# Dense block of a two-layer transformer kernel: sums of inner values all by VectorE, squares by ScalarE, bias rows added in the second half, row statistics one row ahead

## The chip, the cores and the metric

The kernel runs on one core of one Trainium2 chip. The metric is the time of one execution on the device in microseconds (us); before the change it is 3569.39 us, the median of three runs (3567.62 to 3571.59). The engines are named as in the profile: PE is TensorE (matrix products), PEld its weight loads, DVE is VectorE, ACT is ScalarE, POOL is GpSimd, and SP is the queue that issues nearly all transfers (DMAs) between the chip's memory and on-chip memory. Each engine takes its instructions strictly in the order in which the program put them there.

## The reference

All values are float32. Two layers with the same weights run one after the other on x of 2048 rows by 640:

```python
x = x + attention(layernorm(x), wqkv, wo)          # 32 heads of 20
x = x + dense(layernorm(x), w1, b1, w2, b2)

def dense(x, w1, b1, w2, b2):                      # w1: 640 x 1536, w2: 1536 x 640
    h = x @ w1 + b1
    r = where(h > 0, h, 0)
    return (r * r) @ w2 + b2
```

`layernorm` takes a row's mean and variance off and has no weights of its own. So the inner values of the dense part are the squares of what the rectifier lets through, and the bias b2 is a row that is added to every output row.

## The kernel before, in words

PE's operands here are of the type float32r. The kernel splits every operand into a high part (a copy to that type, made by ACT) and a low part (what the copy left out, a subtraction by DVE), and makes three products of each: high-high, high-low, low-high. `split_to` (L322) issues the two instructions.

A layer has three stages: projections to queries, keys and values (`qkv`), `attention`, and what follows here. `add_heads` multiplies the attention's output with wo for four blocks of 512 rows and adds the rows. Then come eight calls of `mlp`, called **blocks** below: `fh` 0 and 1 are the two halves of the 1536 inner columns (first half, second half), and `qb` 0 to 3 are the blocks of 512 rows. The order is fh 0 with qb 0 to 3, then fh 1 with qb 0 to 3; I number them block 0 to block 7 of their layer.

A block has two parts. In the **up** part PE makes six chains of 15 products (L361), one for each 128 inner columns; after each, ACT adds b1 and rectifies (L1454), and DVE squares in place (L1455). After every second chain a **pair** p (0, 1, 2) is complete: `left_operands` makes the left operands of a fast matrix product with seven products in place of eight: sums of quarters of the two squared tiles (L1434 to L1437, four instructions that depend on one another, two for s1 and two for s2), and the splits into high and low of a quarter (`ha`), of the second tile (`h`) and of the sums (`hs`, twice: s1 and s2). In the **y** part PE runs 126 products (L1481) of these operands with w2. It begins with 36 products that need pairs 0 and 1 alone, then takes pair 2: first six products with `ha`, then with s1, with h, and the rest. DVE adds each result to the rows (L1500), 14 instructions.

Beside its own work a block carries **side** work: `side()` is called before the chains, after each of the six chains, once more, and after each of the 14 additions, and each call pops one list of steps that `plan` filled by number (`put(gen, -1, 0, 2)` runs the next step of a generator at those places; -1 is the place ahead of the chains). Two generators matter. `turn_out` normalises four tiles of 128 rows for a later block: statistics (L312, L313 on DVE, then two tiny instructions on POOL, L315 and L316, the second a power), normalisation on DVE (L320), a transposing step on DVE (L1387), and a store to the transposed buffer `d_t` (four DMAs). `turn_in` loads that buffer as columns and splits it (L1403, L1404). In blocks 0 and 1 of both layers `turn_out` runs for a block two further on, and in blocks 5, 6 and 7 of the first layer for the second layer's projections. In block 7 of the first layer the last four row tiles stay on chip: `rows_3` holds their normalised values, which PE transposes early in the second layer (L476).

The order of each engine's instructions is the order in which this Python code issues them; what is waited for follows from the data and from the buffers: 11 buffers for rows (`xtile`) and 42 for operands (`slot`), each reused once its last reader is done. Bias rows: in the first half the four row tiles of x come from the layer's middle rows, and POOL adds b2 to each (L1466); in the second half they come from `d_half`, what the first half stored.

## Time and profile before

| what | us |
|---|---|
| median of three runs | 3569.39 |
| the profiled execution, whole | 3574.83 |
| its span from first to last instruction | 3573.0 |
| PE busy in the span | 3461.2 |
| DVE, ACT, POOL busy | 2864.7, 2640.3, 975.4 |
| the eight blocks of layer one, from their first product | 1416.9 to 1805.7 |
| the eight blocks of layer two | 3204.2 to 3569.6 |
| a block without a wait on PE (layer two, block 5) | 38.9 |

The profiled execution is one run; it took 5.4 us more than the median, and what is summed below is a difference within it. A row of the view of stretches gives a stretch's borders and length, then for PE, PEld, DVE, ACT and POOL the busy time with the number of instructions, then the clock that PE was granted (1.00 is full), the busy share of the transfer engines and GB/s. A row of the timeline gives start, duration, engine, line, operation and tiles, and in brackets the idle time just before it with what ended it. A row of the view of groups gives the count, the busy time and the mean duration in ns, then the idle time before.

### The profile page before, as it was taken

To read this page: it belongs to the slowest core of one execution; us is meant where nothing else is said; L and a number is where in the kernel's file an instruction comes from. 1 tells how busy PE (TensorE), PEld (TensorE's weight loads), DVE (VectorE), ACT (ScalarE), POOL (GpSimd) and SP (SyncE) were. 2 spreads that over 40 slices of the span, in tenths; PEclk is the share of its full clock that TensorE was granted. 3 is DMA by queue.
4 is the path that set the end of the run, shared out by engine and by line. 5 is a ranking of instruction groups with operands and counts; after the bars stand their busy time and mean duration, and the time that the engine had idled before them with its cause. 6 is when DMAs were issued, how large, how long until landed. Compare 5 with 4: busy or idle time off the path is not lost. (4 is left out here: it accounts for less than half of the span.)

```text
span 3573.0 us, 70330 instructions
## 1 busy us (share of the span) xinstructions
PE 3461.2 (97%) x26202; PEld 2163.7 (61%) x26202; DVE 2864.7 (80%) x5341; ACT 2640.3 (74%) x4266; POOL 975.4 (27%) x1128
## 2 busy tenths in 40 slices
PE   9999999999999999799999999999999999997999
PEld 7896444444444438688879964444444444386888
DVE  8888999999999954565668889999999999545654
ACT  3778999999999990232237799999999999902322
POOL 6531355412221120331244201221122211203321
PEclk9999999999999999899999999999999999998999
DMA  9866555422221148756587652222222111487552
GB/s 307 287 223 176 174 170 165 153 65 79 63 54 31 51 152 272 236 207 226 159 268 274 208 158 79 67 85 65 65 79 63 53 31 51 148 275 226 198 220 107
DMA packets 405512, 533.22 MB, mean 149 GB/s; under 512 B 179764, under 2 KB 227380, under 8 KB 405168
## 3 DMA queue, kind: packets, MB, share of 16 engines
q1 hardware_dynamic: 404352, 526.35, 47.0%
q8 instruction: 206, 3.38, 0.4%
q10 hardware_dynamic: 816, 2.36, 0.2%
q14 instruction: 138, 1.13, 0.1%
HBM read 316.59 MB, written 211.98 MB: 148 GB/s over the span
## 5 line engine op out<-in xcount | busy, mean ns | idle before, releaser
L561 DVE TENSOR_REDUCE mx<-banks 128x1 f32<-128x512 f32 x2096 | 1429.0, 686 | 139.5 <-PE banks L549 39.7
L549 PE MATMUL banks<-k,q 60*128 60x512 f32 (+1 forms) x4488 | 1312.3, 371 | 2.0 <-DVE v L445 1.9
L549 PEld LDWEIGHTS banks<-k,q 60*128 60x128 f32 x4488 | 715.0, 184 | 832.2 <-DVE mx L596 725.3
L684 ACT ACTIVATE e<-banks 128x512 f32<-128x512 f32 x1988 | 1194.2, 601 | 16.7 <-PE banks L676 3.6
L690 PE MATMUL banks<-e,vg 128*32 128x512 f32 x8192 | 1093.5, 606 | 1.5 <-ACT e L1295 1.5
L676 PE MATMUL banks<-q,k 62*128 62x512 f32 x3968 | 1074.4, 421 | 0.6 <-DVE mx L617 0.6
L686 ACT ACTIVATE e<-banks 128x1024 f32<-128x1024 f32 x990 | 1007.1, 1017 | 0.0
L596 DVE TENSOR_REDUCE mx<-banks 128x2 f32<-128x512 f32 x928 | 633.0, 682 | 3.3 <-PE banks L549 3.3
L676 PEld LDWEIGHTS banks<-q,k 62*128 62x128 f32 x3968 | 579.9, 184 | 53.8 <-ACT e L684 52.0
L617 DVE CUSTOM_DVE_ANT_0 rl<-banks,rl 128x512 f32<-128x512 f32 x536 | 349.9, 689 | 78.2 <-PE banks L549 56.9
L399 PE MATMUL banks<-xnT,wqk 64*128 64x512 f32 x2400 | 374.6, 394 | 2.3 <-DVE x L1500 1.3
L609 ACT ACTIVATE rl<-banks 128x512 f32<-128x512 f32 x538 | 295.8, 595 | 101.3 <-PE banks L549 85.5
L361 PE MATMUL banks<-xnT,w 128*128 128x512 f32 x1440 | 335.6, 394 | 8.2 <-DVE xnT L1404 8.2
L690 PEld LDWEIGHTS banks<-e,vg 128*32 128x32 f32 x8192 | 161.2, 108 | 261.8 <-issue 257.7
L399 PEld LDWEIGHTS banks<-xnT,wqk 64*128 64x128 f32 x2400 | 297.5, 186 | 32.0 <-issue 2.2
L361 PEld LDWEIGHTS banks<-xnT,w 128*128 128x128 f32 x1440 | 273.0, 190 | 66.3 <-DVE xnT L1404 10.1
L339 POOL CAST mr<-nt 128x32 fp32r<-128x32 f32 x64 | 13.5, 211 | 1086.9 <-DVE nt L643 1086.9
L1454 ACT ACTIVATE r<-banks,b_t 128x512 f32<-128x512 f32 x96 | 64.0, 686 | 301.7 <-PE banks L361 282.2
L734 POOL TENSOR_TENSOR few<-few,minus_t 128x16 f32<-128x16 f32 x62 | 179.9, 2901 | 200.5 <-DMA few<-d_s 200.3
L399 PE MATMUL banks<-wv,xnT 64*128 64x320 f32 x1920 | 209.9, 307 | 0.7 <-ACT mark_t L401 0.7
L399 PEld LDWEIGHTS banks<-wv,xnT 64*128 64x128 f32 x1920 | 202.2, 186 | 1.8 <-ACT mark_t L401 1.4
L549 PE MATMUL banks<-kd,q 60*128 60x512 f32 x538 | 193.4, 397 | 0.0
(111 smaller groups left out, 2969.9 us busy)
## 6 DMA issues: line engine op xcount, KB each, us to landing
q<-d_qk SPq DMA_DIRECT2D x240, 240.0 KB
d_qk<-ev SPq DMA_DIRECT2D x80, 512.0 KB
k<-d_qk SPq DMA_DIRECT2D x152, 240.0 KB
w<-d_w SPq DMA_DIRECT2D x56, 480.0 KB
x<-d_x SPq DMA_DIRECT2D x84, 320.0 KB
d_qk<-ev SPq DMA_DIRECT2D x80, 256.0 KB
d_xn<-xnT SPq DMA_DIRECT2D x40, 512.0 KB
xnT<-d_xn SPq DMA_DIRECT2D x40, 512.0 KB
```

The lines of the kernel that those rows point to most:

```text
L361: nc.tensor.matmul(dst, a, b, start=(n == 0), stop=(n == last))
L399: m = nc.tensor.matmul(ch["dst"][:, :width], *pair, start=first, stop=last)
L549: return nc.tensor.matmul(dst, q_t[t][b : b + 60, p, sub * P : (sub + 1) * P], k_t[t // NQB, c][b : b + 60, p, keys], start=True, stop=True,)
L561: nc.vector.tensor_reduce(maxima(t)[:, 2 * par + p, sub, c : c + 1], dst, axis=AX.X, op=ALU.max)
L596: r = nc.vector.tensor_reduce(maxima(t)[:, p : p + 3 : 2, sub, c if not half else column(t, p, sub)], bank.rearrange("q (r k) -> q r k", r=2),
L609: nc.scalar.activation(res, dst, AF.Relu)
L617: nc.vector.tensor_tensor_reduce(out=r, in0=dst, in1=r, scale=1.0, scalar=LEAST, op0=ALU.add, op1=ALU.max, accum_out=maxima(t)[:, 2 * par ...
L676: nc.tensor.matmul(dst, k_t[t // NQB, kt // 4][b : b + 62, p, (kt % 4) * P : (kt % 4 + 1) * P], q_t[t][b : b + 62, p, :], start=True, stop ...
L684: nc.scalar.activation(es[h], dst, AF.Exp, scale=SCALE)
L686: nc.scalar.activation(es[pair], banks[:, 1:3, :], AF.Exp, scale=SCALE)
L690: nc.tensor.matmul(acc[32 * h : 32 * h + 32, :], v_t[t // NQB, kt // 8][:, kt % 8, 32 * h : 32 * h + 32], es[h], start=(kt == 0), stop=(kt ...
L734: nc.gpsimd.tensor_tensor(few, few, minus_t, op=ALU.pow)
```

## The change

- **Sums.** The four sums of a pair (L1434 to L1437) are issued on DVE for every pair. Before, only pair 2 had them on DVE, and pairs 0 and 1 had them on POOL.
- **Squares.** The square is an activation on ACT (`Square`, in place, right after the rectifier) in place of DVE's product.
- **The quarter `ha`.** Its split is issued right after the first chain of a pair (`upper`), no longer among the pair's other splits; the three other splits take their buffers one by one.
- **Bias rows.** `tensor_add(x, x, b2_t)` on POOL runs in the second half's blocks, no longer in the first half's.
- **Statistics.** `turn_out` takes the statistics of row tile i+1 before it normalises tile i, and has 7 steps in place of 10; the places in `plan` are new. In blocks 0 and 1 the four tiles are done by side place 4 (before, the fourth's normalisation stood at place 13) and stored by place 5; the first two rows of the following `turn_out` are loaded at place 17 in place of 18. In blocks 5 to 7 of layer one the last store stands at place 7.
- **`rows_3`.** In the first layer's block 7 the statistics of tiles 0 and 1 stay at their place; all normalisations, and the statistics of tiles 2 and 3, stand behind the last addition.

```diff
+        mvs = [stats(xs[0])]
+        yield
         for i in range(4):
             if y is not None:
                 store(i - 1)
-            mv = stats(xs[i])
-            yield
-            normalise(nc.vector, xs[i], mv)
+            if i < 3:
+                mvs.append(stats(xs[i + 1]))
+            normalise(nc.vector, xs[i], mvs[i])
             y = xtile("y")
             nc.vector.transpose(y, xs[i])
...
-        def left_operands(p, r, h):
-
-            eng = nc.vector if p == 2 else nc.gpsimd
+        def upper(p, r):
+
             if p % 2 == 0:
                 ops["a", p // 2] = slot([P, 2, QB], F32R, "ha")
             a = ops["a", p // 2][:, :, p % 2 * w : p % 2 * w + w]
-            ops["s1", p] = slot([P, 2, QB], F32R, "hs")
-            ops["s2", p] = slot([P, 2, QB], F32R, "hs")
-            ops["h", p] = slot([P, 2, QB], F32R, "h")
+            split_to(a[:, 0, :], a[:, 1, :], r[:, :w])
+
+        def left_operands(p, r, h):
+
             s = slot([P, 2, 2, w], F32, "s")
             a11, a21, a12, a22 = r[:, :w], r[:, w:], h[:, :w], h[:, w:]
-            eng.tensor_add(s[:, 0, 0, :], a21, a22)
-            eng.tensor_sub(s[:, 0, 1, :], s[:, 0, 0, :], a11)
-            eng.tensor_sub(s[:, 1, 0, :], a12, s[:, 0, 1, :])
-            eng.tensor_sub(s[:, 1, 1, :], a11, a21)
-            split_to(a[:, 0, :], a[:, 1, :], a11)
-            for x, y in (("h", h), ("s1", s[:, 0]), ("s2", s[:, 1])):
-                x = ops[x, p]
+            nc.vector.tensor_add(s[:, 0, 0, :], a21, a22)
+            nc.vector.tensor_sub(s[:, 0, 1, :], s[:, 0, 0, :], a11)
+            nc.vector.tensor_sub(s[:, 1, 0, :], a12, s[:, 0, 1, :])
+            nc.vector.tensor_sub(s[:, 1, 1, :], a11, a21)
+            for key, y in (("h", h), ("s1", s[:, 0]), ("s2", s[:, 1])):
+                x = ops[key, p] = slot([P, 2, QB], F32R, "hs")
                 y = y if y is h else y.rearrange("p a t -> p (a t)")
                 split_to(x[:, 0, :], x[:, 1, :], y)
...
             nc.scalar.activation(r, dst, AF.Relu, bias=b1_t[:, f : f + 1])
-            nc.vector.tensor_mul(r, r, r)
+            nc.scalar.activation(r, r, AF.Square)
             if low:
                 left_operands(p, top, r)
                 top = None
             else:
                 top = r
+                upper(p, r)
...
                 x = row_tile(d_half if fh else x_mid, qb * 4 + n - 1)
-                if not fh:
+                if fh:
                     nc.gpsimd.tensor_add(x, x, b2_t)
...
                     if final and not last:
-                        rows_3.append((x, stats(x)))
-                        if i:
-                            rows_3[i - 1] = to_normal(*rows_3[i - 1])
+                        rows_3.append((x, stats(x) if j == 4 else None))
...
+        for i, (x, mv) in enumerate(rows_3[:]):
+            if i == 3:
+                rows_3[i] = x, stats(x)
+            else:
+                rows_3[i] = to_normal(x, mv or stats(x))
+        x = None
...
-                    (out_0, range(10)), (out_1, range(9, 19)), (in_0, (12, 16, 17, 18, 19, 20))
+                    (out_0, range(7)), (out_1, (9, 10, 11, 13, 15, 17, 18)), (in_0, (8, 12, 14, 16, 18, 19))
...
-                put(outs.pop(0), -1, -1, 0, 0, 2, 2, 4, 13, 14)
+                put(outs.pop(0), -1, -1, 0, 2, 4, 5)
...
-                put(outs[0], 18)
+                put(outs[0], 17)
...
-                at = (6, 8, 9) if qb + 1 == NQB else (13, 15, 16)
-                put(turn_out(d_t[1 + qb], rows_of(x_e, qb - 1)), -1, 0, 0, 2, 2, 4, 4, *at)
+                put(turn_out(d_t[1 + qb], rows_of(x_e, qb - 1)), -1, 0, 0, 2, 4, 6, 7)
```

How this moves instructions is best seen in the built programs. In the lists `r` is a squared tile, `s` the sums, `ha`, `h` and `hs` the split operands, `x` a row tile, `bst` and `mv` its statistics, `y` its transposed or normalised form; the numbers tell tiles apart. New line numbers are two higher than old ones from L1385 on.

**DVE, layer one, block 5, the last pair of the up part.** Before:

```order
L1455 TENSOR_TENSOR r_18262<-r_18262 128x512
L312 BN_STATS bst_18271<-x_18136 128x6 x2
L313 BN_AGGR mv_18272<-bst_18271 128x2
L320 TENSOR_SCALAR x_18136<-x_18136,mv_18272 128x640
L1387 STREAM_TRANSPOSE y_18279<-x_18136 128x640
L1455 TENSOR_TENSOR r_18296<-r_18296 128x512
L1434 TENSOR_TENSOR s_18303<-r_18262,r_18296 128x256
L1435 TENSOR_TENSOR s_18303<-s_18303,r_18262 128x256
L1436 TENSOR_TENSOR s_18303<-r_18296,s_18303 128x256
L1437 TENSOR_TENSOR s_18303<-r_18262 128x256
L325 TENSOR_TENSOR ha_18299<-r_18262,ha_18299 128x256
L325 TENSOR_TENSOR h_18302<-r_18296,h_18302 128x512
```

With the change:

```order
L325 TENSOR_TENSOR ha_18263<-r_18260,ha_18263 128x256
L312 BN_STATS bst_18273<-x_18208 128x6 x2
L313 BN_AGGR mv_18274<-bst_18273 128x2
L320 TENSOR_SCALAR x_18134<-x_18134,mv_18199 128x640
L1389 STREAM_TRANSPOSE y_18281<-x_18134 128x640
L1436 TENSOR_TENSOR s_18301<-r_18260,r_18298 128x256
L1437 TENSOR_TENSOR s_18301<-s_18301,r_18260 128x256
L1438 TENSOR_TENSOR s_18301<-r_18298,s_18301 128x256
L1439 TENSOR_TENSOR s_18301<-r_18260 128x256
L325 TENSOR_TENSOR hs_18306<-r_18298,hs_18306 128x512
L325 TENSOR_TENSOR hs_18309<-s_18301,hs_18309 128x512
L325 TENSOR_TENSOR hs_18312<-s_18301,hs_18312 128x512
```

The two squares are gone from DVE, `ha` stands ahead of the row work, and the normalisation (L320) uses an `mv` of an earlier step, no longer the one just above it.

**DVE, layer two, the beginning of block 1.** Before:

```order
L312 BN_STATS bst_35143<-x_35112 128x6 x2
L313 BN_AGGR mv_35144<-bst_35143 128x2
L320 TENSOR_SCALAR x_35112<-x_35112,mv_35144 128x640
L1387 STREAM_TRANSPOSE y_35151<-x_35112 128x640
L1455 TENSOR_TENSOR r_35170<-r_35170 128x512
L312 BN_STATS bst_35177<-x_35114 128x6 x2
L313 BN_AGGR mv_35178<-bst_35177 128x2
L320 TENSOR_SCALAR x_35114<-x_35114,mv_35178 128x640
L1387 STREAM_TRANSPOSE y_35185<-x_35114 128x640
L1455 TENSOR_TENSOR r_35204<-r_35204 128x512
L325 TENSOR_TENSOR ha_35207<-r_35170,ha_35207 128x256
L325 TENSOR_TENSOR h_35210<-r_35204,h_35210 128x512
```

With the change:

```order
L312 BN_STATS bst_35139<-x_35098 128x6 x2
L313 BN_AGGR mv_35140<-bst_35139 128x2
L312 BN_STATS bst_35146<-x_35100 128x6 x2
L313 BN_AGGR mv_35147<-bst_35146 128x2
L320 TENSOR_SCALAR x_35098<-x_35098,mv_35140 128x640
L1389 STREAM_TRANSPOSE y_35154<-x_35098 128x640
L325 TENSOR_TENSOR ha_35176<-r_35173,ha_35176 128x256
L312 BN_STATS bst_35183<-x_35156 128x6 x2
L313 BN_AGGR mv_35184<-bst_35183 128x2
L320 TENSOR_SCALAR x_35100<-x_35100,mv_35147 128x640
L1389 STREAM_TRANSPOSE y_35191<-x_35100 128x640
L1436 TENSOR_TENSOR s_35213<-r_35173,r_35210 128x256
```

The statistics of the third row tile (`x_35156`) now stand ahead of the first pair's sums; before, they stood behind that pair's splits.

**DVE, layer one, the end of block 7** (`xnT_19392` is the next stage's first split). Before:

```order
L1414 TENSOR_SCALAR y_19270<-x_18961,mv_19232 128x640
L1404 TENSOR_TENSOR xnT_19119<-xnT_19119 128x512
L1500 TENSOR_TENSOR x_19033<-banks,x_19033 128x320
L1500 TENSOR_TENSOR x_19053<-banks,x_19053 128x320
L1500 TENSOR_TENSOR x_19033<-banks,x_19033 128x320
L312 BN_STATS bst_19313<-x_19033 128x6 x2
L313 BN_AGGR mv_19314<-bst_19313 128x2
L1414 TENSOR_SCALAR y_19320<-x_18981,mv_19264 128x640
L1500 TENSOR_TENSOR x_19053<-banks,x_19053 128x320
L312 BN_STATS bst_19335<-x_19053 128x6 x2
L313 BN_AGGR mv_19336<-bst_19335 128x2
L1414 TENSOR_SCALAR y_19342<-x_19033,mv_19314 128x640
```

With the change:

```order
L1502 TENSOR_TENSOR x_19038<-banks,x_19038 128x320
L1502 TENSOR_TENSOR x_19062<-banks,x_19062 128x320
L1416 TENSOR_SCALAR y_19330<-x_18964,mv_19232 128x640
L1416 TENSOR_SCALAR y_19332<-x_18987,mv_19264 128x640
L312 BN_STATS bst_19334<-x_19038 128x6 x2
L313 BN_AGGR mv_19335<-bst_19334 128x2
L1416 TENSOR_SCALAR y_19341<-x_19038,mv_19335 128x640
L312 BN_STATS bst_19343<-x_19062 128x6 x2
L313 BN_AGGR mv_19344<-bst_19343 128x2
L1416 TENSOR_SCALAR y_19358<-x_19062,mv_19344 128x640
L325 TENSOR_TENSOR xnT_19392<-banks,xnT_19392 128x512
```

The additions (L1500, now L1502) no longer have statistics and normalisations between them, and each normalisation of tiles 2 and 3 stands right behind the statistics that it uses.

## The prediction

> **What bounds the kernel now.** The change moves instructions in the dense blocks and in the rows around them alone, so I read the view of stretches first, one stretch for each block with a loss, and one without.
>
> ```profile
> 1416.90:1491.60 74.70, 48.85 (x219) 41.55 (x218) 41.06 (x77) 13.71 (x24) 18.49 (x22) 0.77 0.77 230
> 1491.60:1539.60 48.00, 42.29 (x218) 37.46 (x218) 33.37 (x61) 12.99 (x23) 17.64 (x20) 0.93 0.62 184
> 1539.60:1580.90 41.30, 39.58 (x218) 35.36 (x217) 26.04 (x41) 13.12 (x23) 14.59 (x12) 1.00 0.43 160
> 1580.90:1624.50 43.60, 41.24 (x219) 36.93 (x218) 24.15 (x36) 10.52 (x18) 14.89 (x12) 0.96 0.98 372
> 1663.40:1710.00 46.60, 41.51 (x218) 37.57 (x217) 28.50 (x56) 10.40 (x18) 10.55 (x16) 0.93 0.60 170
> 1710.00:1757.20 47.20, 42.12 (x219) 38.25 (x218) 30.80 (x60) 13.48 (x23) 10.54 (x16) 0.93 0.68 195
> 1757.20:1807.00 49.80, 41.17 (x217) 36.78 (x216) 35.96 (x74) 16.59 (x28) 14.87 (x23) 0.97 0.64 178
> 3204.20:3280.10 75.90, 48.17 (x219) 41.23 (x218) 41.14 (x77) 13.71 (x24) 18.49 (x22) 0.78 0.75 225
> 3280.10:3328.90 48.80, 41.62 (x218) 36.77 (x217) 33.34 (x61) 12.99 (x23) 17.57 (x20) 0.97 0.62 181
> 3328.90:3371.80 42.90, 41.18 (x219) 36.97 (x218) 26.14 (x41) 13.12 (x23) 14.59 (x12) 0.96 0.43 154
> 3371.80:3413.80 42.00, 39.64 (x218) 35.32 (x217) 24.00 (x36) 10.51 (x18) 15.08 (x12) 1.00 1.01 388
> 3452.80:3491.70 38.90, 38.90 (x218) 35.37 (x217) 19.38 (x36) 10.63 (x18) 7.58 (x8) 1.00 0.39 136
> ```
>
> The last row is a block in which PE never waits: 38.9 us. Every other block pays its length less 38.9. Layer one: 35.8, 9.1, 2.4, 4.7 (blocks 0 to 3), 7.7, 8.3, 10.9 (5 to 7; the last up to the next stage's first product). Layer two: 37.0, 9.9, 4.0, 3.1. Together 132.9 us, all that the change can win. Part is idle PE, part a clock below 1.00 after it: with 46.6 us and 41.51 busy, block 5 loses 5.1 by waiting and 2.6 by slow products.
>
> Next the timeline of block 5, PE first, then DVE.
>
> ```profile
> 1663.39 20.59 PE L361 MATMUL banks<-xnT,w 128*128 128x512 f32 x90
> ...
> 1689.14 0.56 PE L1481 MATMUL banks<-w,ha 128*128 128x320 f32 x2
> 1694.79 1.43 PE L1481 MATMUL banks<-w,ha 128*128 128x320 f32 x4 [5.09 <-DVE ha L325]
> ```
>
> ```profile
> 1687.97 0.68 DVE L1455 TENSOR_TENSOR r<-r 128x512 f32<-128x512 f32 x1
> 1688.57 0.88 DVE L312 BATCH_NORM_STATS2 bst<-x 128x6 f32<-128x320 f32 x2
> 1689.48 0.21 DVE L313 BATCH_NORM_AGGREGATE mv<-bst 128x2 f32<-128x12 f32 x1
> 1690.62 0.61 DVE L320 TENSOR_SCALAR x<-x,mv 128x640 f32<-128x640 f32 x1 [0.93 <-POOL mv L316]
> 1691.27 0.84 DVE L1387 STREAM_TRANSPOSE y<-x 128x640 f32<-128x640 f32 x1
> 1692.04 0.65 DVE L1455 TENSOR_TENSOR r<-r 128x512 f32<-128x512 f32 x1
> ...
> 1694.32 0.42 DVE L325 TENSOR_TENSOR ha<-r,ha 128x256 fp32r<-128x256 f32 x1
> ```
>
> PE begins pair 2 at 25.75 us of the block (1689.14 less 1663.39) and stands until `ha` of pair 2 is there. The bound is DVE's order: between the two squares stand a row's statistics, a 0.93 us round trip to POOL, the normalisation and the transposing step. Everything of pair 2, on ACT too, waits for them.
>
> **The change, part by part.** Prices come from the undisturbed block (3452.8 to 3491.7), the view of groups:
>
> ```profile
> L1454 ACT ACTIVATE r<-banks,b_t 128x512 f32<-128x512 f32 x6 | 4.1, 688 | 21.0 <-PE banks L361 20.9
> L324 ACT CAST hs<-s 128x512 fp32r<-128x512 f32 x6 | 3.7, 621 | 6.1 <-POOL s L1435 2.9 <-POOL s L1437 2.7 <-DVE s L1435 0.3
> L1455 DVE TENSOR_TENSOR r<-r 128x512 f32<-128x512 f32 x6 | 4.1, 690 | 6.5 <-ACT r L1454 6.4
> L325 DVE TENSOR_TENSOR hs<-s,hs 128x512 fp32r<-128x512 f32 x6 | 4.1, 689 | 5.1 <-ACT hs L324 5.1
> L1435 DVE TENSOR_TENSOR s<-s,r 128x256 f32<-128x256 f32 x1 | 0.4, 424 | 0.0
> L1435 POOL TENSOR_TENSOR s<-s,r 128x256 f32<-128x256 f32 x2 | 2.1, 1068 | 0.2
> ```
>
> *Squares.* DVE loses six instructions of 0.69 us a block (4.1 us). ACT gains six. No row shows a square on ACT; the nearest are the copy (0.62) and the rectifier with its bias (0.69), and I take 0.65, as it has no tile of biases. ACT then works 10.6 + 3.9 = 14.5 of 38.9 us. This hides beside PE except behind the last chain, where it takes the place of DVE's square. The Trainium skill ("ScalarE: Activation LUTs", the rules for kernel authors) speaks against this part: an element-wise product belongs on VectorE. It gives an ACTIVATE with immediate operands 186 ns + 0.833 ns an element, an estimate of 613 ns for 512. The rows show no dearer engine here (0.62 to 0.69 against 0.69), so the sum is the same by either, and DVE, not ACT, is late.
>
> *Sums.* DVE gains eight instructions a block at 0.42 (3.4 us), about what it lost. The four of a pair take 1.6 us (from 1692.04 + 0.65 to 1694.32, with their waits) where one alone takes POOL 1.07. Before, ACT's `hs` copies waited for POOL; now they wait for DVE. Behind them on ACT stands the next rectifier, and behind that PE's banks, of which eight cover several chains.
>
> *Row statistics ahead.* Nothing is added; the wait for POOL's power (0.93) falls under the next statistics (1.09).
>
> *A block with row work in the second half (5, 6, 7).* Chains end every 3.43 us (20.59/6). The fifth ends at 17.2, `ha` is done near 19.7 (rectify, square, copy, subtract), the row work of side 4 takes 0.88 + 0.21 + 0.61 + 0.84 = 2.5, until 22.2. The last chain's square is there at 20.6 + 0.7 + 0.65 = 22.0. Sums until 23.8, `h` low 24.5, s1 low 25.2. PE wants s1 at 25.75 + 6 products of 0.147 ((38.9 - 20.4)/126) = 26.6. Slack 1.4: no wait. I leave 0.5 us for a collision with POOL. Gains: 7.2 and 7.8.
>
> *Blocks 2 and 3*, no row work: s1 low near 25.0; all of 2.4 + 4.7 + 4.0 + 3.1 = 14.2 goes.
>
> *Blocks 1.* Here the moved statistics meet a transfer. SP (layer two) and what it brings:
>
> ```profile
> 3285.82 1.20 SPq L76 DMA_DIRECT2D x<-d_x  x1
> ...
> 3290.94 1.46 SPq L76 DMA_DIRECT2D x<-d_x  x3
> ```
>
> ```profile
> 3296.76 3.08 POOL L1466 TENSOR_TENSOR x<-x,b_t 128x640 f32<-128x640 f32 x2 [3.25 <-DMA x<-d_x]
> ```
>
> The third tile's load is issued 5.7 us into the block, and the flight of such a load is 5.3 to 5.8 (3290.94 to 3296.76, a bias row of the three), so it lands near 11.0. DVE's statistics of it now stand ahead of pair 0's sums and wait from about 5.8; behind them on DVE queue all the pairs, and PE waits for those. From 11.0 DVE has three row steps (1.1 + 1.45, 1.1 + 1.45, 1.45), three sets of sums (4.8), two sets of three splits (4.0), `ha` twice with ACT's copy (1.9), and the last `h` and s1 (1.3): 18.55, until 29.6. PE wants it at 26.6, so 3 us are lost, and 9.1 + 9.9 - 6 = 13.0 is won. A flight of 3.7 wins 3 more in all, one of 8.1 (below) 5 less.
>
> *Blocks 0.* Layer two:
>
> ```profile
> 3224.07 1.29 SPq L76 DMA_DIRECT2D x<-d_x  x2
> ...
> 3232.99 0.36 SPq L76 DMA_DIRECT2D x<-d_x  x1
> 3235.78 7.04 SPq L76 DMA_DIRECT2D d_t<-y  x4
> ```
>
> ```profile
> 3232.20 0.89 DVE L312 BATCH_NORM_STATS2 bst<-x 128x6 f32<-128x320 f32 x2 [18.28 <-DMA x<-d_x]
> ```
>
> ```profile
> 3264.78 1.44 PE L1481 MATMUL banks<-w,ha 128*128 128x320 f32 x4 [2.65 <-DVE ha L325]
> ```
>
> The first two tiles land at 3232.2, 8.1 us after their issue and 18.28 after DVE wanted them; the same bytes are ahead of them in the queue after the change, so I keep that. The third is issued at 3232.99; with the same 8.1 it lands at 3241.1 (with 5.3, 3238.3). Then again 18.55: 3259.7. From its last wait PE needed 3280.1 - 3264.78 = 15.3 for 90 products; from s1 on, 84 take about 14.4, so 3274.1: 6 us won. With layer one 12 (5 more with the shorter flight; nothing if the landing moves by 6).
>
> *The end of layer one's block 7.* Its 10.9 falls by the waits, but `rows_3` now comes behind the last addition, and PE transposes it soon:
>
> ```profile
> 1809.51 4.00 POOL L1404 TENSOR_TENSOR xnT<-xnT 128x512 fp32r<-128x512 f32 x3
> ```
>
> ```profile
> 1813.40 1.09 PE L476 MATMUL banks<-ident,y 128*128 128x128 f32 x8
> ```
>
> PE wants the rows 6.4 us after the next stage begins. DVE has two normalisations, statistics, POOL's power (queued behind those subtractions, which I expect to end near 5.5), a normalisation, and the same once more: near 10. I take a stall of 3.5 and 1.4 for banks and weights as before: 6.0 won. Bounds: 10.9 and 3.
>
> *The rest.* The stage before the blocks only gets its row work shuffled; its cover is the transfers that set when block 0's rows land. I cost it at nothing; without that cover it is worth no more than block 0's range. The second half's bias additions hide beside DVE.
>
> **The sum.** 15.0 (5, 6) + 14.2 + 13.0 + 12 + 6 = 60 us of 132.9. The profiled execution's 3574.8 becomes 3514.6; it lies 5.4 above the median, so the median 3569.4 becomes 3509.
>
> **The rivals.**
>
> *Less: DVE and POOL collide.* Four bias additions a block now stand beside DVE's sums.
>
> ```profile
> L1466 POOL TENSOR_TENSOR x<-x,b_t 128x640 f32<-128x640 f32 x32 | 55.4, 1752 | 13.3 <-DMA x<-d_x 10.8 <-issue 2.5
> L1455 DVE TENSOR_TENSOR r<-r 128x512 f32<-128x512 f32 x96 | 80.6, 844 | 68.6 <-ACT r L1454 67.9
> ```
>
> DVE's square takes 0.84 on average and 0.69 in a block without bias additions, so something stretches it. If each of eight second-half blocks loses the slack and about 1.5 us more, 12 go back: 3521. Against it: most rows land early, while pair 2 is still far. The Trainium skill ("SBUF — State Buffer", "Who interferes with whom") has a VectorE instruction with two on-chip inputs block wholly against a GpSimd one that reads there; those two rows agree. Chance 0.14.
>
> *Less: blocks 0 and block 7's end give nothing*, since the landing sets both: 60 - 18 = 42, so 3527. For it stand the 18.28 us. Chance 0.13.
>
> *More: the loads fly faster once DVE no longer holds the queue's stores.* Blocks 0 gain 5 more, blocks 1 lose nothing (6 more), block 7 another 5: 3493. Against it is the share of 0.75 in block 0. Chance 0.14.
>
> *Slower: the row ahead holds DVE.* One mechanism: the statistics of a later tile stand ahead of the operands in seven blocks. If that tile flew as long as DVE's longest wait (18.28) in all, blocks 0 and 1 would lose 13 more each (52) and blocks 5 to 7 about 6 each (18): 3579. It decides from a flight of about 16 us; the rows show 5.3 to 8.1. Chance 0.04.
>
> *The change does not do what it says*, for instance because ACT's square proves slow: 0.02, near 3569.
>
> The forecast keeps 0.53. About 0.2% (7 us) is what a measurement tells from no change here. Faster by more: 0.93; within: 0.03; slower: 0.04. The range runs from just beyond the case of more, 3489, to a little beyond the two cases of less, 3536.
>
> **What would show it.** Right: in blocks 2, 3, 5 and 6 no wait of PE for `ha`, and lengths near 39; in blocks 1 one wait for an `hs` of pair 2, near 3 us, and a wait of DVE's L312 for x<-d_x ahead of the first sums; in blocks 0 a length near 70. Wrong: PE waiting for `hs` in second-half blocks, squares on ACT above 0.8 us, or blocks 1 as long as before.

## The result, and the profile after

The changed kernel takes 3519.15 us (median of 4 runs, 3517.54 to 3521.56) against 3570.49 for the kernel before on the same chip: ratio 0.9857, 95% interval 0.9840 to 0.9874, 51 us less. The profiled execution's span went from 3573.0 to 3515.7 us, 57.3 less; the 6 us between the two figures are that the profiled execution of before lay 4.3 above its median and the one of after 1.6 below. In one experiment below, squares alone, one of the four executions took 6367.7 us, nearly twice the other three and for no cause that a trace shows; the ratio given there is of the three.

The view of stretches of the changed kernel, in the columns of the one before the prediction (stretch, length, busy times of PE, its weight loads, DVE, ACT and POOL, the granted clock, the DMA share, GB/s): blocks 5, 6, 7 of layer one, then blocks 0, 1 and 2 of layer two.

```profile
1639.40:1683.30 43.90, 40.94 (x218) 36.89 (x217) 32.01 (x58) 14.34 (x24) 10.68 (x12) 0.96 0.64 180
1683.30:1727.40 44.10, 41.29 (x218) 36.87 (x217) 34.51 (x62) 17.43 (x29) 10.34 (x12) 0.96 0.73 209
1727.40:1774.00 46.60, 42.33 (x219) 36.77 (x217) 38.54 (x73) 20.47 (x34) 16.61 (x20) 0.96 0.68 188
...
3174.60:3238.20 63.60, 44.07 (x218) 38.13 (x218) 34.64 (x73) 17.42 (x29) 3.81 (x8) 0.81 0.83 253
3238.20:3278.70 40.50, 39.36 (x217) 35.30 (x217) 29.98 (x63) 17.45 (x29) 3.81 (x8) 1.00 0.73 212
3278.70:3317.60 38.90, 38.90 (x218) 35.37 (x217) 21.14 (x43) 17.16 (x29) 0.00 (x0) 1.00 0.47 169
```

Block 2 is now at the floor of 38.9, and so are all of blocks 2 to 4 and layer two's 5 to 7. Blocks 1 pay 2, blocks 0 still 24, and blocks 5 to 7 of layer one 5 and more, in which POOL is busy for 10 us and more.

Each length below runs from a block's first product to the next block's; block 7 of layer one is counted to its own last product; "stage" is the stage ahead of the blocks.

| | before | changed |
|---|---|---|
| layer one: stage | 72.8 | 75.7 |
| blocks 0, 1, 2, 3 | 74.7, 48.0, 41.3, 43.6 | 63.1, 41.0, 38.9, 38.9 |
| blocks 4, 5, 6, 7 | 38.9, 46.6, 47.2, 48.5 | 38.9, 43.9, 44.1, 45.2 |
| layer two: stage | 72.6 | 75.4 |
| blocks 0, 1, 2, 3 | 75.9, 48.8, 42.9, 42.0 | 63.6, 40.5, 38.9, 38.9 |

The rows give 62.5 us in the blocks and take 5.7 in the two stages: 56.8 of the span's 57.3.

Why block 5 is not at the floor is read from three engines. PE's timeline of it:

```profile
1639.41 20.59 PE L361 MATMUL banks<-xnT,w 128*128 128x512 f32 x90
...
1665.12 1.04 PE L1483 MATMUL banks<-w,ha 128*128 128x320 f32 x6
1668.33 0.56 PE L1483 MATMUL banks<-w,hs 128*128 128x320 f32 x2 [2.17 <-ACT hs L324]
1669.68 13.83 PE L1483 MATMUL banks<-w,hs 128*128 128x320 f32 x82 [0.79 <-DVE hs L325]
```

DVE's timeline of the same block:

```profile
1648.68 1.69 DVE L1436 TENSOR_TENSOR s<-r,r 128x256 f32<-128x256 f32 x1
1650.40 1.68 DVE L1437 TENSOR_TENSOR s<-s,r 128x256 f32<-128x256 f32 x1
1652.12 0.42 DVE L1438 TENSOR_TENSOR s<-r,s 128x256 f32<-128x256 f32 x1
...
1658.00 1.69 DVE L1436 TENSOR_TENSOR s<-r,r 128x256 f32<-128x256 f32 x1
...
1661.46 2.66 DVE L325 TENSOR_TENSOR hs<-s,hs 128x512 fp32r<-128x512 f32 x2
...
1666.78 0.38 DVE L1436 TENSOR_TENSOR s<-r,r 128x256 f32<-128x256 f32 x1
```

And POOL's:

```profile
1648.52 3.28 POOL L1468 TENSOR_TENSOR x<-x,b_t 128x640 f32<-128x640 f32 x2
...
1657.84 1.57 POOL L1468 TENSOR_TENSOR x<-x,b_t 128x640 f32<-128x640 f32 x1
1661.48 2.10 POOL L1468 TENSOR_TENSOR x<-x,b_t 128x640 f32<-128x640 f32 x1 [2.07 <-DMA x<-d_half]
```

The wait for `ha` is gone; in its place PE waits 2.96 us for s1 of pair 2. Beside each of POOL's four bias additions DVE takes 1.3 to 1.4 us longer than its like (1.69 for 0.42; 2.66 for two splits that take 1.29 elsewhere). That makes 5.2 us in DVE's order, whose only gap between the first sums and pair 2 is one of 0.57, so the sums of pair 2 begin 27.4 us into the block. Of the 5.0 us by which the block is over the floor, 2.96 are PE's wait; the other 2.0 are slower products, as PE is busy for 40.94 us in place of 38.90, at a granted clock of 0.96.

In block 0 of layer two DVE's and PE's timelines show what the 63.6 us are:

```profile
3197.99 0.89 DVE L312 BATCH_NORM_STATS2 bst<-x 128x6 f32<-128x320 f32 x2 [18.17 <-DMA x<-d_x]
...
3208.21 0.89 DVE L312 BATCH_NORM_STATS2 bst<-x 128x6 f32<-128x320 f32 x2 [6.36 <-DMA x<-d_x]
```

```profile
3201.90 0.64 PE L1483 MATMUL banks<-w,ha 128*128 128x320 f32 x1 [5.57 <-DVE ha L325]
3214.64 2.77 PE L1483 MATMUL banks<-w,ha 128*128 128x320 f32 x9 [12.11 <-ACT ha L324]
...
3226.04 12.29 PE L1483 MATMUL banks<-w,hs 128*128 128x320 f32 x82 [0.38 <-DVE hs L325]
```

DVE stands for rows that it is to treat ahead of pair 0's operands, twice, and PE stands behind it.

### The profile page after: what moved, and what is told of

It is laid out like the page before. It is cut to its first block, busy times and chain, and to the rows that moved or that the text cites. A ratio compares the mean times of both kernels' runs of the same rounds, so it can differ in the third digit from the quotient of the medians.

```text
span 3515.7 us, 70233 instructions
## 1 busy us (share of the span) xinstructions
PE 3440.0 (98%) x26202; PEld 2144.1 (61%) x26202; DVE 2846.9 (81%) x5373; ACT 2704.6 (77%) x4362; POOL 857.7 (24%) x1000
## 4 chain that ended last, share of the span: by engine, by line
PE 91%; DVE 4%; DMA 3%; ACT 1%; issue 1%; SPq 0%; POOL 0%; DVEq 0%; ACTq 0%; POOLq 0%
PE banks L690 29%; PE banks L549 19%; PE banks L676 14%; PE banks L399 11%; PE banks L361 9%; PE banks L1483 7%; DMA x<-d_x 1%; DVE bst L312 1%; PE banks L1288 1%; DMA d_t<-y 1%; DVE y L1389 1%; DVE x L320 1%; DVE hs L325 0%; DVE s L1436 0%; DVE s L1437 0%
## 5 line engine op out<-in xcount | busy, mean ns | idle before, releaser
L1483 PE MATMUL banks<-w,hs 128*128 128x320 f32 x1728 | 271.6, 316 | 14.7 <-DVE hs L325 7.7
L339 POOL CAST mr<-nt 128x32 fp32r<-128x32 f32 x64 | 13.4, 210 | 1088.2 <-DVE nt L643 1088.2
L1483 PEld LDWEIGHTS banks<-w,hs 128*128 128x128 f32 x1728 | 262.3, 193 | 20.8 <-DVE hs L325 11.0
```

The lines of the kernel that those rows point to most:

```text
L1483: nc.tensor.matmul(dst[:, :HALF], t[:, hx, c : c + P], w_2.piece(j, p, hw), start=start and p == 0 and (hx, hw) == THREE[0], stop=stop and ...
```

## The experiments

The times below are medians beside the kernel before on the same chip (3569.3 to 3570.6). The lengths are read from each run's trace, one execution each, as in the table above.

### Is it the bias rows? They are left out, or put back

**Left out.** This kernel leaves out the addition of b2 and is otherwise the changed one.

```diff
             if 1 <= n <= 4:
                 x = row_tile(d_half if fh else x_mid, qb * 4 + n - 1)
-                if fh:
-                    nc.gpsimd.tensor_add(x, x, b2_t)
                 xs.append(x)
```

> The changed kernel without POOL's additions of the bias rows (L1468); what is left out is exactly these additions, 32 of 1.75 us. Theory A, a collision: in blocks 5 to 7 of layer one DVE's sums take 1.69 us in place of 0.42 because POOL adds bias rows beside them. Then blocks 5, 6 and 7 fall from 43.9, 44.1 and 46.6 us to 39 to 40, 39 to 40 and about 42.5, the other blocks stay, and the kernel is about 13 us (11 to 15) below the changed one: 3506. Theory B, a chain too long: the row work, the sums and the splits are more than DVE can do ahead of PE's first s1 product, with POOL or without. Then blocks 5 and 6 stay at 43 to 44, and the time is 3516 to 3520.

Measured: 3503.7 us, ratio 0.9816 (0.9799 to 0.9832), 15.4 below the changed kernel. Blocks 5, 6 and 7 are 38.9, 38.9 and 40.0 us, which is 15.4 less in these three; block 0 of layer one and layer two's stage are about 2 us longer each, the rest stayed within 1. (That the blocks' 15.4 equals the difference of the medians is a coincidence; the profiled executions differ by 13.4.) In the timelines of block 5, DVE's first, then PE's:

```profile
1650.39 0.38 DVE L1436 TENSOR_TENSOR s<-r,r 128x256 f32<-128x256 f32 x1
1650.81 0.42 DVE L1437 TENSOR_TENSOR s<-s,r 128x256 f32<-128x256 f32 x1
...
1663.91 0.38 DVE L1436 TENSOR_TENSOR s<-r,r 128x256 f32<-128x256 f32 x1
```

```profile
1641.13 20.59 PE L361 MATMUL banks<-xnT,w 128*128 128x512 f32 x90
...
1667.71 12.48 PE L1481 MATMUL banks<-w,hs 128*128 128x320 f32 x84
```

The sums of pair 2 begin 22.8 us into the block, and PE passes to s1 without a wait. Every sum of DVE is back at 0.38 to 0.43. Theory A holds, and B falls: the chain fits ahead of PE when POOL is still.

**Back in the first half** (`if not fh:` in place of `if fh:`).

> The changed kernel with the bias rows added in the first half, as before the change: that part alone undone. Theory A (collision): blocks 5 to 7 give back the same 13 us as without the additions; blocks 2 and 3, which have no row work, lose nothing; blocks 1, which have it, lose 3 to 5 us each, and blocks 0, where PE waits for landed rows, 0 to 3 each. Sum: 3513 to 3522. Theory B (chain too long): no block moves by more than 1 us: 3517 to 3521.

Measured: 3526.4 us, ratio 0.9878 (0.9863 to 0.9892): 7 above the changed kernel, and above the 3513 to 3522 of theory A. Blocks 5 to 7 give 15.3 back, about as foreseen, but blocks 0 lose 5.3 and 5.2 (68.4 and 68.8), blocks 1 lose 4.7 and 5.5, and blocks 3 lose 1.1 and 1.9. DVE and PE in block 1 of layer one:

```profile
1502.81 4.05 DVE L325 TENSOR_TENSOR hs<-s,hs 128x512 fp32r<-128x512 f32 x2
...
1509.51 1.66 DVE L1436 TENSOR_TENSOR s<-r,r 128x256 f32<-128x256 f32 x1
1511.21 1.64 DVE L1437 TENSOR_TENSOR s<-s,r 128x256 f32<-128x256 f32 x1
```

```profile
1513.55 0.56 PE L1483 MATMUL banks<-w,hs 128*128 128x320 f32 x2 [3.64 <-ACT hs L324]
```

Theory A again, with two misses: I had expected blocks 0 to lose 0 to 3, as PE there waits for landed rows, and blocks 3, which have no row work, to lose nothing. Behind the landing DVE has a full chain, and each stretch in it is paid whole. The bias rows cost about 5 us wherever a block has row work, and 0 to 1.9 in a block without: layer two's second half has none, which is why the change's place for them is the better one.

### What sets blocks 0?

**Block 2's four rows loaded ahead of the stage's last weight loads.**

```diff
-            for f in loads[qb]:
-                f()
             if qb + 1 == NQB:
                 next(outs[0])
+            for f in loads[qb]:
+                f()
+            if qb + 1 == NQB:
                 all_steps()
...
-            xs.extend(read(i) for i in range(2))
+            xs.extend(read(i) for i in range(first))
```

(`first` is a new argument of `turn_out`, 4 here; the later reads fall away.)

> The changed kernel with the loads of block 2's four rows, which DVE treats at the start of block 0, issued ahead of the last weight loads and stores of the stage before, all four together (before: two behind them, the third and fourth as DVE gets on). Theory C, the landing sets blocks 0: DVE there waits 18.17 us for the first tiles and 6.36 for the third; with these gone PE's 5.57 and 12.11 us of waiting for ha fall away for the most part, and blocks 0 fall from 63.1 and 63.6 us to 43 to 53: 3483 to 3499 in all. Theory D, the queue only changes places: SP's queue and the DMA engines (0.75 busy there) are the limit, so the weight loads or the dense block's own rows come late by what the rows gain, and the time stays within 5 us of 3519.

Measured: 3503.2 us, ratio 0.9813 (0.9798 to 0.9828), 16 below the changed kernel. Blocks 0 are 56.1 and 58.8 us, 7.0 and 4.8 less; blocks 1 are 0.7 and 0.8 less. Layer two, DVE and PE:

```profile
3181.87 0.89 DVE L312 BATCH_NORM_STATS2 bst<-x 128x6 f32<-128x320 f32 x2 [13.51 <-DMA x<-d_x]
```

```profile
3185.79 0.41 PE L1483 MATMUL banks<-w,ha 128*128 128x320 f32 x1 [0.83 <-DVE ha L325]
3192.08 2.77 PE L1483 MATMUL banks<-w,ha 128*128 128x320 f32 x9 [5.88 <-ACT ha L324]
```

Theory C has the direction and, in the blocks, half the size or less: the rows still land 17.8 us into the block (3181.87 less 3164.04), and after that DVE's chain is what it was.

**The turned rows of block 0 read back later**, at the sides of before.

```diff
-(in_0, (8, 12, 14, 16, 18, 19))
+(in_0, (12, 16, 17, 18, 19, 20))
```

> The changed kernel with block 0's turned rows read back at the sides where they were read before the change (12, 16 to 20 in place of 8, 12 to 19) in the stage before the blocks; the row steps stay spread as changed. Theory E: the five loads of xnT (3.77 us on SP), which the change put ahead of the loads that DVE's statistics wait for (18.64 us of idle time until 3161.35), make PE wait 3.11 us there. Then the stage falls from 75.4 to about 72.6 us in both layers. But the rows that block 0 waits for land when they did, so blocks 0 grow by about 2.8 each: within 2 us of 3519. Theory F: the stage's loss has another cause (DVE's row steps now stand two together between PE's banks): the stage keeps 75 to 76 us, and the time is also near 3519, or above by up to 4 since block 0's operands come later.

Measured: 3520.4 us, ratio 0.9861 (0.9846 to 0.9876): no difference from the changed kernel. It tests the 5.7 us that the two stages lost, whose rows in the changed kernel, layer two, are one of DVE and one of PE:

```profile
3161.35 0.89 DVE L312 BATCH_NORM_STATS2 bst<-x 128x6 f32<-128x320 f32 x2 [18.64 <-DMA x<-d_x]
```

```profile
3162.89 2.46 PE L361 MATMUL banks<-wo,ot 128*128 128x320 f32 x15 [3.11 <-DVE x L1355]
```

With the later reading PE's timeline there is:

```profile
3161.52 2.46 PE L361 MATMUL banks<-wo,ot 128*128 128x320 f32 x15 [1.00 <-DVE x L1355]
...
3176.41 2.19 PE L361 MATMUL banks<-xnT,w 128*128 128x512 f32 x4 [3.04 <-issue]
```

The wait of 3.11 falls to 1.00, as theory E has it, but a wait of 3.04 opens ahead of block 0's first product (3.48 in layer one), so the stages do not fall to 72.6: they are 75.7 and 76.4 us, and blocks 0 are 1 us longer. What ended the new wait the profile doesn't name. In both layers DVE had just stood 5.5 us for a row tile, and PE goes on 0.1 us after the addition (L1355) that stood behind that tile in DVE's order. So the loss moves and does not go, and this run doesn't show what makes the stages longer.

### Each part alone, and undone

**Squares alone**, on the kernel before:

```diff
-            nc.vector.tensor_mul(r, r, r)
+            nc.scalar.activation(r, r, AF.Square)
```

> The kernel before with the squares on ACT, nothing else of the change. Theory G, the parts add up: each part takes its own work off DVE's way, and the gains of the parts alone sum to the 51 us of the whole. Then this part, which takes six instructions of 0.69 us a block off DVE, gives 15 to 25 us: 3545 to 3555; blocks 2 and 3, where DVE has no row work, lose their 2.4 to 4.7 us of waits. Theory H, the parts need each other: POOL's sums (1.07 us each) and the row work on DVE keep the operands late, so this alone gives less than 10: 3560 to 3570.

**Sums alone**, on the kernel before:

```diff
-            eng = nc.vector if p == 2 else nc.gpsimd
+            eng = nc.vector
```

> The kernel before with the sums of pairs 0 and 1 on DVE, nothing else of the change. If the parts add up, what is left for the sums and the bias rows is 51 - 42 + 5 = 14 us of gain; the bias rows' place was worth 7, so the sums alone give about 7: 3559 to 3566. If DVE is the late engine, eight more instructions of 0.42 us a block ahead of ha make it later: 3572 to 3595, slower than before, and the sums gain only once the squares are gone from DVE.

**The row part alone** (the changed `turn_out`, the sides and `rows_3`) on the kernel before:

> The kernel before with the row statistics one row ahead, the new sides and the later to_normal, and with squares, sums and bias rows as they were. Theory G: seven blocks have row work, four waits of 0.6 to 0.9 us for POOL's power fall away in each, and blocks 0 start their rows sooner by the 4.6 us that the landing moved: 15 to 25 us, 3545 to 3555. Theory H: the statistics of the third tile stand ahead of the operands in blocks 0 and 1 and DVE still has the squares, so what the waits for POOL give is lost in blocks 1: within 8 us of before, 3562 to 3578.

**The row part undone** (these three as before, the dense part as changed):

> The changed kernel with the row statistics, their sides and to_normal as before: the dense part alone (sums on DVE, squares on ACT, bias rows in the second half). Theory G: it loses what the row part gives alone, 15 to 25 us: 3534 to 3544, with blocks 0 near 70 us or longer and the stage ahead of them back at 72.7. Theory H: blocks 5 and 6 get shorter or stay (the row work stood at later sides, 13 to 16 in block 5, where DVE has time), blocks 0 grow by 5 to 6 each: 3525 to 3534.

**Squares undone**: the changed kernel with `tensor_mul` on DVE again.

> The changed kernel with the squares back on DVE: that part alone undone. Theory I, the squares are most of the gain whatever stands beside them (alone they gave 42 us): 3555 to 3567, with PE waiting for ha and hs of DVE in blocks 0 to 3 and 5 to 7. Theory J, the squares gave so much alone because POOL still had its sums, and with the sums on DVE each engine has less to offer: DVE now has squares and sums, so it is over 26 us of work ahead of s1 and it costs more than 50: above 3569.

| | us | ratio to before (95%) | blocks 0, 1, 2, 3 of layer one | 5, 6, 7 |
|---|---|---|---|---|
| before | 3570 | | 74.7, 48.0, 41.3, 43.6 | 46.6, 47.2, 48.5 |
| squares alone | 3527.9 | 0.9885 (0.9869 to 0.9902) | 70.4, 43.3, 38.9, 39.9 | 39.5, 39.6, 45.7 |
| sums alone | 3536.1 | 0.9899 (0.9883 to 0.9916) | 73.9, 44.9, 39.5, 40.3 | 42.9, 41.5, 46.9 |
| row part alone | 3575.6 | 1.0021 (1.0012 to 1.0031) | 76.1, 52.0, 41.3, 43.4 | 43.8, 43.8, 45.1 |
| squares undone | 3541.4 | 0.9921 (0.9906 to 0.9936) | 65.1, 44.3, 38.9, 38.9 | 48.0, 47.9, 48.9 |
| row part undone | 3512.8 | 0.9846 (0.9831 to 0.9861) | 63.2, 38.9, 38.9, 38.9 | 45.3, 45.1, 48.1 |
| changed | 3519.2 | 0.9857 (0.9840 to 0.9874) | 63.1, 41.0, 38.9, 38.9 | 43.9, 44.1, 45.2 |

Of these expectations one held, the second theory of the row part alone; the other four runs fell outside both theories. Squares alone give 42 us, far more than either had; sums alone give 33, where one theory had a loss; 42 + 33 - 5 + 7 (the bias rows' place, as measured in the changed kernel) is 77, and the whole gives 51. The parts neither add up nor need each other: in part they replace each other. The view of groups shows how: DVE's splits of s1 and s2 in the kernel before, with the idle time ahead of them;

```profile
L325 DVE TENSOR_TENSOR hs<-s,hs 128x512 fp32r<-128x512 f32 x96 | 71.9, 762 | 82.0 <-ACT hs L324 82.0
```

with squares alone;

```profile
L325 DVE TENSOR_TENSOR hs<-s,hs 128x512 fp32r<-128x512 f32 x96 | 85.7, 914 | 35.9 <-ACT hs L324 32.9
L325 DVE TENSOR_TENSOR h<-r,h 128x512 fp32r<-128x512 f32 x48 | 50.7, 1057 | 0.0
```

and with sums alone:

```profile
L325 DVE TENSOR_TENSOR hs<-s,hs 128x512 fp32r<-128x512 f32 x96 | 67.3, 742 | 0.0
```

The squares were 80.6 us of DVE's work; POOL's sums held DVE for 82.0 us, standing still behind ACT's copies of what POOL had not yet summed. Over 16 blocks that is 5 us a block either way, and the blocks other than 0 that lost anything had lost 2 to 10. So whichever goes first wins most of what PE waited for, and the second finds less. Squares undone says it from the other end: put in last, the squares are worth 22 us (3541.4 less 3519.2), not 42. The early split of `ha` was not run by itself; it is in the last three rows of the table, and no run shows what it is worth.

With squares alone 35.9 us of that standing are left, and the splits take longer (914 and 1057 ns) as POOL's sums now fall beside them: in block 5 of layer one a split of 128x512 takes 1.22 us beside POOL's sums, and 0.69 once POOL is done. My charge against sums alone, eight more DVE instructions a block, is paid by the idle time that goes with POOL's sums.

The row part alone is slower than before by 0.21% (interval 0.12 to 0.31): it gains 2.8, 3.4 and 3.4 in blocks 5 to 7 and 4.0 in layer two's block 0, and loses 1.4 in layer one's, 4.0 and 2.3 in blocks 1 and 1.8 and 5.2 in the stages. Undone, it leaves 3512.8, 6 us under the changed kernel (the ratios' intervals overlap, the blocks say where): blocks 1 come down to 38.9 both times and the stages to 71.4 and 73.5, against 1.4, 1.0 and 2.9 more in blocks 5 to 7. In block 1 of layer one with the row part undone, DVE and PE read:

```profile
1481.29 0.61 DVE L320 TENSOR_SCALAR x<-x,mv 128x640 f32<-128x640 f32 x1 [0.93 <-POOL mv L316]
```

```profile
1504.81 12.48 PE L1481 MATMUL banks<-w,hs 128*128 128x320 f32 x84
```

The wait for POOL's power that the row ahead was to hide is there and costs this block nothing, once squares and POOL's sums are gone.

### Versions

Three versions put the causes together. The first keeps the early loads and moves block 0's row work behind pair 1's operands:

```diff
-                put(outs.pop(0), -1, -1, 0, 2, 4, 5)
+                put(outs.pop(0), *((-1, -1, 0, 2, 4, 5) if qb else (3, 3, 4, 5, 6, 7)))
...
-                put(turn_out(d_t[1 + qb], rows_of(x_e, qb - 1)), -1, 0, 0, 2, 4, 6, 7)
+                put(turn_out(d_t[1 + qb], rows_of(x_e, qb - 1)), -1, 0, 0, 2, *((13, 15, 16) if qb == 1 else (4, 6, 7)))
...
-                if fh:
+                if fh != (not last and qb > 1):
                     nc.gpsimd.tensor_add(x, x, b2_t)
```

> The changed kernel with four edits against the causes found so far: the early four loads; in block 0 the row work behind pair 1's operands, not ahead of pair 0's; bias rows of layer one's blocks 2 and 3 added in the first half, where there is no row work to collide with; in block 5 three of the row steps at sides 13 to 16, where DVE has only the additions of y. If DVE's order behind the landing is what blocks 0 still pay for, they fall from 56 and 59 us to 40 to 45; blocks 5, 6 and 7 fall to 39 to 41: 3519 - 16 (loads) - 28 - 5 - 5 - 6 = 3459, between 3455 and 3475. If the queue is the limit in blocks 0 (the dense block's own rows and the next turned rows come late), they stay above 52 and the time above 3480.

Measured: 3492.7 us, ratio 0.9786 (0.9771 to 0.9800), a miss for the hoped 3455 to 3475. Blocks 0 are 49.8 and 51.0, blocks 5 to 7 are 40.3, 40.3 and 40.0, but blocks 1 grew to 44.6 and 43.8: in layer one's DVE stands 5.47 us for the load of a third tile ahead of pair 0's sums, and PE behind it. In blocks 0 PE now waits for the additions of y (the longest wait is 5.67 us in layer one), and those wait on DVE first behind the moved rows and then for the block's own rows:

```profile
1450.55 0.85 DVE L1389 STREAM_TRANSPOSE y<-x 128x640 f32<-128x640 f32 x1
1453.93 0.49 DVE L1502 TENSOR_TENSOR x<-banks,x 128x320 f32<-128x320 f32 x1 [2.53 <-DMA x<-d_x]
```

So both of its theories have a part in blocks 0, DVE's order and the late rows.

The second moves that work out of block 0 altogether. The four reads together, the row steps of blocks 5 and 6 at sides 13 to 16 and the bias rows of layer one's block 3 in the first half (so that its block 7 has none) are not repeated here:

```diff
-        outs = [turn_out(d_t[0], rows_of(x_m, 2))]
+        outs = []
...
-            if not fh and qb + 2 < NQB:
-                put(outs.pop(0), -1, -1, 0, 2, 4, 5)
-            if not fh and qb + 3 < NQB:
-                outs.append(turn_out(d_t[(qb + 1) % 2], rows_of(x_m, qb + 3)))
+            if outs:
+                put(outs.pop(0), -1, -1, -1, 0, 0, 1)
+            if not fh and qb + 2 < NQB:
+                outs.append(turn_out(d_t[qb % 2], rows_of(x_m, qb + 2), 4))
                 put(outs[0], 17)
```

> The changed kernel with the row work of blocks 0 and 1 moved one block on (to the start of blocks 1 and 2, all four rows loaded at side 17 of the block ahead), three row steps of blocks 5 and 6 at sides 13 to 16, and the bias rows of layer one's block 3 added in the first half. If DVE's order behind the landing is all that blocks 0 lose by, blocks 0 fall from 63 to 39 to 43 us, blocks 1 and 2 lie at 39 to 42, blocks 5 to 7 at 40 to 41: 3519 - 43 - 13 = 3463, between 3455 and 3475. If the dense block's own rows land late too (SP's queue behind the stage's stores), blocks 0 stay near 50 as in the version before: 3480 to 3490.

Measured: 3469.1 us, ratio 0.9717 (0.9703 to 0.9732), inside the first range, though blocks 0, at 46.7 and 44.8, are above their 39 to 43; blocks 1 and 2 are at 38.9, blocks 5 to 7 at 40.2, 41.0 and 40.9. DVE in block 0 of layer two:

```profile
3155.34 0.43 DVE L1436 TENSOR_TENSOR s<-r,r 128x256 f32<-128x256 f32 x1 [2.56 <-ACT r L1456]
...
3179.13 0.49 DVE L1502 TENSOR_TENSOR x<-banks,x 128x320 f32<-128x320 f32 x1 [6.71 <-DMA x<-d_x]
```

The operands now wait for ACT's square alone. What is left is the block's own rows, late for y. The third version asks for the last two weight pieces behind them:

```diff
-        for s in range(12, w_2.n):
-            w_2.load(0, s)
...
+            if not fh and not qb:
+                for s in range(12, w_2.n):
+                    plan[6].append(lambda s=s: w_2.load(0, s))
```

> The shifted version with the last two weight pieces of the dense block's second product asked for at side 5 of block 0, no longer ahead of it. In the shifted version PE's only waits in blocks 0 are 4.48 and 4.25 us for the additions of y, which wait for the block's own rows (6.71 us, x<-d_x); their four loads stood on SP behind those two weight loads. If the queue's order is what makes them late, they are issued 3 us sooner, blocks 0 fall from 46.7 and 44.8 to about 42, and the time by 5 to 8 us to 3461 to 3464. If the landing is set by the bytes ahead of them, or the weight pieces now come late themselves, it stays at 3466 to 3474.

Measured: 3466.5 us, ratio 0.9707 (0.9691 to 0.9723), the fastest here, 104 us under the kernel before. SP's rows of the second and then of the third version, layer two:

```profile
3166.21 2.08 SPq L76 DMA_DIRECT2D w<-d_w  x2
3169.10 4.10 SPq L76 DMA_DIRECT2D x<-d_x  x4
```

```profile
3165.37 3.97 SPq L76 DMA_DIRECT2D x<-d_x  x4
...
3170.33 1.56 SPq L76 DMA_DIRECT2D w<-d_w  x2
```

Blocks 0 come to 41.9 and 41.9, as the queue's order would have it. The time fell by 2.6 only, not by 5 to 8, and lies in the other theory's range: the two were measured on different chips (the kernel before took 1.3 us more on the second), the intervals of the two ratios overlap, and in the profiled execution layer one's stage began 2.6 us later and was 1.6 longer. Why is open.

## Why the prediction was right, and where not

The forecast was 3509, in a range of 3489 to 3536, and 3519 was measured: faster, as forecast, by 51 us where 60 were predicted. Its sum, term by term, against the changed kernel's profile:

| term | predicted | measured |
|---|---|---|
| blocks 5 and 6 | 15.0 | 5.8 |
| blocks 2 and 3 | 14.2 | 14.2 |
| blocks 1 | 13.0 | 15.3 |
| blocks 0 | 12 | 23.9 |
| end of block 7 | 6.0 | 3.3 |
| the stage ahead of the blocks | 0 | -5.7 |
| sum | 60 | 56.8 |

(Block 7 is counted to its own last product; to the next stage's first product, as the prediction counts, it is 4.1.) The total is nearer than its terms. Blocks 5 and 6, block 7 and the stage were put 17.6 us too high, blocks 0 and 1 14.2 too low, and that these nearly cancel is luck.

*Blocks 5 and 6.* The step that failed is "I leave 0.5 us for a collision with POOL", and a sign that the prediction had named for being wrong came with it, PE's wait for `hs` (2.17 and 0.79 us). The rest of it stands: without the bias additions pair 2's sums begin 22.8 us into block 5, where the working had 22.0 for their square and 22.2 for DVE, and the block loses nothing. The collision was 5.2 us of DVE's time in a block whose slack the working put at 1.4. The rival "DVE and POOL collide" had the mechanism; its price was 1.5 us in each of eight second-half blocks, and the runs show 5.0 to 5.2 in the three with row work and nothing in the five without. That its sum of 12 was near the 15.4 is luck, by that count, and so is its 3521, nearer than the forecast. The counterargument to it, that most rows land early while pair 2 is far, was wrong: a stretch early in the block does no harm only if DVE has a gap behind it, and here it has next to none. Layer two's block 5 has gaps: one of DVE's sums takes 1.67 us there beside POOL (3404.82), and the block stays at 38.9.

The Trainium skill ("SBUF — State Buffer", "Who interferes with whom") says that a VectorE instruction with two on-chip inputs and a GpSimd one that reads there contend for one read port, and that the one that comes second is held for the whole of the other. This case's trace agrees: 1.69 us for 0.42 beside additions of 1.6 us, and 0.38 to 0.43 without them; the DVE sum that began at 1648.68, 0.16 us behind POOL's addition, ended 0.3 us behind it.

*Squares.* Taken at 0.65 us; the row is this, ACT in the changed kernel:

```profile
3179.77 0.63 ACT L1456 ACTIVATE r<-r 128x512 f32<-128x512 f32 x1
```

An estimate by the Trainium skill's "ScalarE: Activation LUTs" ("What ACT_TABLE_LOAD costs") was 613 ns, 3% under it. The Trainium skill's rule there ("Rules for kernel authors") that an element-wise product belongs on VectorE, which spoke against this part, is not borne out here, where the two engines take nearly the same (0.63 and 0.69 us) and VectorE is the one that is late: that part alone gave 42 us.

*Sums.* The working put them down as a near even trade on DVE, 4.1 us against 3.4, and found the gain in the order of DVE's work. What it did not price is DVE's 82.0 us of standing behind ACT's copies, and through them behind POOL, which end with POOL's sums. It did no harm to the total, as that was built from the waits of PE, block by block.

*Blocks 1.* The third tile's load landed 10.6 us into block 1 of layer two (11.0 in the working), DVE stood 4.71 us for it, and from there to the last s1 operand it needed 17.8 us, not 18.55, as in block 0. That is 1.15 of the 3 us that I had charged; the block pays 1.6. That this wait is the row part's own doing is shown by the row part undone: 38.9 in both.

*Blocks 0.* Two assumptions were off, both to the good. "The same bytes are ahead of them in the queue" kept the first landing at 28.0 us; it came at 23.4, of which 2.8 is only that block 0 itself began later, and the third tile's at 33.6 against 36.9. Then 14.4 us for the last 84 products was taken from a stretch in which PE was granted a clock of 0.83; after the change the same stretch is at 1.00 and shows 12.29 for 82. Together with the stage's loss of 5.7, which I had costed at nothing, blocks 0 give 18.2 net where 12 were predicted. The dense part brings that gain: with the row part undone blocks 0 are 63.2 and 64.1. The stage's 5.7 is the second step that failed, "only gets its row work shuffled". That the row part does it is shown: alone it makes the two stages 1.8 and 5.2 us longer, and undone it leaves them at 71.4 and 73.5. Which of its moves does it is open. Block 0's turned rows are now read ahead of loads on SP's queue for which DVE, and behind DVE PE, waits; but with that reading put back the stages stayed at 75.7 and 76.4.

*Block 7.* The stall of 3.5 us at the transposes did not come: `rows_3` was ready. The collision came instead, 5.2 us (45.2 to 40.0 without the bias rows).

*The other rivals.* "Blocks 0 and block 7's end give nothing" was wrong; "the loads fly faster" did not hold for flights (8.0 us for the first two tiles, 3190.04 to 3197.99, as before), only for when they were issued. "The row ahead holds DVE" is real at a small size: it is the 2 us of blocks 1, and alone the row part is 0.2% slower.

## What to carry to other kernels

When PE waits for an engine's operands, add up that engine's instructions, its idle time behind other engines, and its stretches beside GpSimd; a part that removes any one of the three can take the same wait, so price parts together and not one by one. Here a GpSimd addition of 1.6 us beside a full VectorE order cost 1.3 us of it, so place it in stages where VectorE has gaps. Work that waits for a transfer should not stand in an engine's order ahead of work that PE will want: the version that moves 10 us of row work one block on is 50 us faster than the changed kernel, and 35 of them are in blocks 0.

## What was not expected of the hardware

A VectorE addition of 128x256 took four times its length (1.69 for 0.42 us) beside one GpSimd addition of 128x640. The GpSimd ones that began first kept their length (1.57 to 1.64 us); the one that began 0.02 us behind a VectorE split took 2.10. The order on SP's queue counts beside the flight: stores of turned rows took 2.0 to 8.3 us on it for four and 9.8 for twelve, and in the changed kernel four such stores (6.39 us at 3201.57) stand there between the load of block 2's third row tile and the next three row loads, while a load's flight was 8 us.
